# A stored table of places and engines, replaced by another, in a fused attention and gated convolution kernel

## The chip, the cores and the metric

The kernel runs on one core of a Trainium2 chip. The metric is the time of one execution on the device in microseconds (us), as a median of several runs. A profile shows one execution, on the engines PE (matrix products; PEld is its loading of weights), DVE (VectorE), ACT (ScalarE), POOL (GpSimd), and SP, which here issues the transfers (DMAs).

## The reference, cut to what matters

```python
# q, k, v: (8, 8, 576, 64), float32
scores = q @ k.T / 8 + bias                 # bias: (8, 576, 576), the same for each batch
attn = softmax(scores); x = attn @ v        # x joined over the 8 heads: (8, 576, 512)
# bias[h,i,j] = relu(log1p(|i-j|) / log1p(max(i,1)) * w1 + b1) @ w2   (32 hidden units)
gate = sigmoid(causal_conv_of_5_taps(x, conv_w))
out = (gate * (x @ w_val)) @ w_out
```

## The kernel before, in words

The work is cut into 4,041 tasks, each a closure that issues one or a few instructions. It falls into three kinds. **Bias stage**: for 36 bands `b0` to `b35` of 16 rows of the bias, four `relu` tasks per band (one on ACT, L319, the other three on DVE or POOL, L321), products on PE (`bias_mm`, L340), evacuations of the product from PSUM with the constant added (`bias_fin`, on ACT L359 or on DVE L361; one forward and one mirrored piece), and a store to DRAM. **Attention**: 32 pairs `p0` to `p31` of two heads of one batch. A pair has four blocks `c0` to `c3` of 128 queries, and every second pair a block `c4` for the 64 rows that remain of two pairs. A block has `qkm` on PE (L714; `qkr`, L730, for c4), two `logits` on DVE (L760), two `expo` on ACT (L772). Pairs 0 to 5, 24 and 25 normalise the exponentials (`norm`), transpose them on PE (L919) and copy them from PSUM (`tev`, on ACT or DVE). The 24 others split each block into two halves of 16 bits: `top` (copy of the upper half, ACT L197, DVE L199 or POOL L201), `rest` and `rest8` (the subtraction that gives the lower half, 1024 and 128 columns, L220), and then a transposing DMA that SP issues (`swap`, L953, into a tile `t_pt`). `piece` tasks (L986) multiply the transposed block with v. **Gated part**: per batch, `taps`, `conv`, `prod` and `acc` for the convolution, `val` (L1251) and `outp` (L1317) on PE, with their copies and subtractions (`ghi`, `glo`, `ote`) on ACT, DVE or POOL.

What sets the order is no scheduler: the string constant `ORDER`, unpacked, gives for every place of the program the number of a task and the number of its engine among those that the task allows. Each engine gets its instructions in this order and works them off in it; slots of buffers are given out in it too. These lines do it, and the second group is what `bias_fin` allows:

```python
for lo, hi in zip(code[:n], code[n:]):
    t = self.tasks[(lo + 256 * hi) // 4]
    assert not t.done and all(d.done for d in t.deps)
    t.on, t.done = t.engines[lo % 4], True
...
f = add(
    [("A", 0.2 + 0.19 * (hi - lo) / 288), ("V", 0.1 + 0.31 * (hi - lo) / 288)],
    partial(bias_fin, j=j, lo=lo, hi=hi, back=back),
```

Of the kernel before, what the change touches and what calls it, by code (L numbers as in the profile page):

```python
# [1489 lines left out]
```

## Time and profile before

| | before |
|---|---|
| median of 3 runs | 660.95 us (663.14, 660.22, 660.95) |
| span of the profiled execution | 656.1 us |
| median of the runs less this span | 4.85 us |
| PE busy in the span | 618.3 us (94%) |
| DVE busy | 591.6 us (90%) |
| ACT busy | 573.2 us (87%) |
| POOL busy | 496.4 us (76%) |

The span runs from the first to the last instruction of the profiled execution; that execution's own time stands nowhere, so the runs' median is what its 4.85 us around the span are taken from. Busy shares are means over the span: they say which engine has the most work, not which one is waited for in a given stage.

### The profile page before, as it was taken

The page shows a single profiled execution, that of the slowest core. Times are in us where ns is not written, and L with a number is a line of the kernel's source. Part 1 is how long each engine was busy: PE and PEld are TensorE (multiplying, and loading weights), DVE is VectorE, ACT ScalarE, POOL GpSimd, SP SyncE. Part 2 cuts the span into 40 slices and gives each one's busy share as a digit, 9 for nine tenths or more (in the row PEclk, how much of TensorE's full clock was granted, in tenths as well). Part 3 has the DMA queues.
Part 4 walks back from the last instruction along what each step waited for, and adds up shares of the span by engine and source line. Part 5 has one row for each costly group of instructions (what it writes and reads, how often), then busy time and mean ns, then how long its engine had stood idle before and what let it go on. Part 6 is the DMA issues. An engine that isn't in the chain of part 4 may idle for free.

```text
span 656.1 us, 16807 instructions
## 1 busy us (share of the span) xinstructions
PE 618.3 (94%) x6176; PEld 401.5 (61%) x6176; DVE 591.6 (90%) x1594; ACT 573.2 (87%) x1284; POOL 496.4 (76%) x566
## 2 busy tenths in 40 slices
PE   5778999999799999999989999999999999999997
PEld 2223666766566676657556676666676664766673
DVE  7999999999999799899898988998988988899882
ACT  6999999999999999899688998889889877999671
POOL 6576839675798888888888778987878957888630
PEclk9979999999999999999999999999999998999999
DMA  6889957338999999999999999999974999999622
GB/s 193 260 278 344 338 204 212 102 115 149 168 238 195 200 230 197 230 225 199 219 190 233 210 208 212 217 217 181 221 188 116 157 224 170 210 193 172 121 81 96
DMA packets 279106, 129.76 MB, mean 198 GB/s; under 512 B 255600, under 2 KB 255856, under 8 KB 279024
## 3 DMA queue, kind: packets, MB, share of 16 engines
q1 hardware_dynamic: 278880, 128.40, 89.5%
q8 instruction: 48, 0.79, 0.5%
q14 instruction: 34, 0.28, 0.2%
q10 hardware_dynamic: 144, 0.29, 0.1%
HBM read 44.64 MB, written 20.33 MB: 99 GB/s over the span
## 4 chain that ended last, share of the span: by engine, by line
PE 63%; DMA 12%; ACT 10%; POOL 6%; DVE 4%; issue 2%; SPq 1%; DVEq 0%; POOLq 0%; ACTq 0%
PE t_sp L714 16%; PE t_ps L986 13%; PE t_ps L1317 11%; DMA t_pt<-t_d 11%; PE t_ps L1251 10%; PE t_ps L919 5%; POOL t_d L220 4%; ACT t_d L772 3%; ACT t_be L359 2%; PE t_sp L730 2%; DVE t_d L760 2%; PE t_ps L1060 2%; PE t_ps L340 2%; ACT rel L319 2%; ACT t_d L197 1%
## 5 line engine op out<-in xcount | busy, mean ns | idle before, releaser
L220 POOL TENSOR_TENSOR t_d<-t_d,t_d 128x1024 f16<-128x1024 f32 (+1 forms) x178 | 242.8, 1382 | 44.1 <-ACT t_d L197 39.0
L772 ACT ACTIVATE t_d<-t_d,nm 128x576 f32<-128x576 f32 x288 | 221.6, 771 | 22.2 <-DVE nm L760 21.6
L760 DVE CUSTOM_DVE_ANT_0 t_d<-t_sp,bias 128x576 f32<-128x576 f32 x256 | 186.5, 752 | 24.8 <-PE t_sp L714 19.3
L714 PE MATMUL t_sp<-t_qk 64*128 64x288 f32 x1024 | 168.1, 429 | 4.0 <-DVE nm L760 3.4
L986 PE MATMUL t_ps<-t_pt,t_w 128*64 128x256 f16 (+1 forms) x1664 | 122.4, 296 | 8.4 <-DMA t_pt<-t_d 6.0
L714 PEld LDWEIGHTS t_sp<-t_qk 64*128 64x128 f32 x1024 | 95.2, 186 | 49.7 <-DVE nm L760 14.0
L197 ACT CAST t_d<-t_d 128x576 f16<-128x576 f32 x155 | 99.7, 666 | 15.4 <-DMA t_pt<-t_d 9.5
L1251 PEld LDWEIGHTS <-wv 128*128 128x128 f16 x768 | 72.4, 98 | 29.9 <-issue 10.5
L986 PEld LDWEIGHTS <-t_w 128*64 128x64 f16 x1344 | 70.3, 110 | 25.2 <-issue 14.8
L1251 PE MATMUL t_ps<-xh,wv 128*128 128x256 f16 (+1 forms) x480 | 68.4, 286 | 0.0
L1183 DVE SCALAR_TENSOR_TENSOR t_ps<-t_xp,convw,t_ps 128x288 f32<-128x288 f32 x126 | 64.6, 517 | 1.3
L1317 PE MATMUL t_ps<-wo,gh 128*128 128x512 f16 x240 | 59.2, 387 | 0.0
L772 ACT ACTIVATION_READ_ACCUMULATOR t_d<-t_d,nm 128x1 f32 x288 | 55.1, 191 | 0.0
L340 PE MATMUL t_ps<-rel,w 128*32 128x280 f32 (+17 forms) x352 | 40.6, 531 | 11.2 <-ACT t_be L359 6.4
L834 POOL TENSOR_SCALAR t_d<-t_d,rinv 128x576 f32<-128x576 f32 x57 | 42.3, 754 | 10.5 <-DVE rinv L806 9.9
L321 POOL TENSOR_SCALAR rel<-gt,ip,nb 128x560 f32<-128x560 f32 (+11 forms) x17 | 38.7, 2281 | 13.1 <-PE t_ps L340 12.6
L321 DVE TENSOR_SCALAR rel<-gt,ip,nb 128x544 f32<-128x544 f32 (+17 forms) x91 | 46.1, 569 | 0.2
L201 POOL TENSOR_SCALAR t_d<-t_d 128x576 f16<-128x576 f32 x46 | 33.9, 740 | 14.7 <-ACT t_d L772 10.8
L919 PE MATMUL t_ps<-ident,t_d 128*128 128x128 f32 x324 | 43.3, 278 | 1.6 <-POOL t_d L834 0.8
L919 PEld LDWEIGHTS t_ps<-ident,t_d 128*128 128x128 f32 x324 | 35.2, 140 | 13.8 <-issue 5.5
L197 ACT COPY t_pt<-t_ps 128x512 f32<-128x512 f32 (+1 forms) x83 | 36.6, 486 | 4.7 <-PE t_ps L919 4.2
L1317 PEld LDWEIGHTS <-gh 128*128 128x128 f16 x240 | 22.6, 100 | 29.0 <-issue 7.8
(156 smaller groups left out, 1082.4 us busy)
## 6 DMA issues: line engine op xcount, KB each, us to landing
t_qk<-qkd SPq DMA_DIRECT2D x32, 576.0 KB, 4.7
bias_d<-t_be SPq DMA_DIRECT2D x36, 295.5 KB, 4.5
bias<-bias_d SPq DMA_DIRECT2D x16, 576.0 KB, 7.1
out<-t_w SPq DMA_DIRECT2D x32, 256.0 KB, 2.6
t_w<-vd SPq DMA_DIRECT2D x24, 320.0 KB, 3.7
t_w<-vn SPq DMA_DIRECT2D x8, 320.0 KB, 4.4
...
```

What stands on the lines that cost most here:

```text
L197: A.copy(out=out, in_=in_)
L220: (V if e == "V" else G).tensor_tensor(out=out, in0=in0, in1=in1, op=ALU.subtract)
L321: (G if e == "G" else V).tensor_scalar(out=rel[g].t[:, 0:w], in0=src, scalar1=sct[:, mm : mm + 1], scalar2=nb1, op0=ALU.mult, op1=ALU.max,)
L340: T.matmul(pb[32 * g : 32 * g + 32, 0 : y - x], lhsT=w28, rhs=rel[g].t[:, x:y], start=True, stop=True, tile_position=(0, 32 * g),)
L714: T.matmul(ts[a][:, j, 0:hw], lhsT=qk.t[r, c * P : (c + 1) * P], rhs=qk.t[r, x : x + hw], start=True, stop=True,)
L760: V.tensor_tensor_reduce(out=part(c, a).rearrange("p (j f) -> p j f", j=2), in0=sp.t[:, :, 0 : S // 2], in1=bias.rearrange("p (j f) -> p j ...
L772: A.activation(out=part(c, a), in_=part(c, a), func=AF.Exp, bias=nms[c][:, a : a + 1], scale=-1.0, accum_out=sums[c][:, a, 0:1],)
L919: T.transpose(t[:, k * P : (k + 1) * P], es[c].t[:, (k0 + k) * P : (k0 + k + 1) * P], ident)
L986: T.matmul(po.t[r, 0:256], lhsT=vt.t[:, v, r], rhs=pt[:, x, :, :] if tr else pt[:, :, x, :], start=(t == 0 and m == 0), stop=(t == 4 and m ...
L1183: V.scalar_tensor_tensor(out=o, in0=x, scalar=wt, in1=t, op0=ALU.mult, op1=ALU.add)
L1251: T.matmul(pm.t[:, 0:w], lhsT=weights["wv"][wi][:, k, d * P : (d + 1) * P], rhs=xb.t[xi][:, k, 0:w], start=(q == 0 and k == 0), stop=(q == ...
L1317: T.matmul(pm.t, lhsT=gb.t[gi][:, k, o : o + P] if o < 256 else gx.t[gi][:, k, :], rhs=weights["wo"][wi][:, k, :], start=(q == 0 and k == ...
```

## The change

Only the constant `ORDER` differs; no task, tile or pool is changed. Of its text one line of each:

```diff
 ORDER = (
-    'c-mE10cbL3nx6mvCuWjNl1UsBlT7}MagvP5Bu<jiOp?i8yV%7p7VP1IJ?vr+yLgK|>|zgl*uz~cSg?l$d$`~o7VP1FxQl!EFLtqD!5;2m7jN;v1-sbAJ?vq@1$VLF9`}A@ckk|<`M&RcpZ9s+_jBf(ZzjPAx+#*B$FFbT3`exQ*Y!JJ0B=j3MwspPf)U=<Y&-j{S384Ylr0p?rHb7Vi@O|eCEd<$Ae2gHpAS}R;lbE5Y-V!A'
...
+    'c-nPW4{RdWnaA0I9ou7jY!B<PJ=lXiwg-D`#_O?nY|rLMMJiGeiJVA9P9&lya-t`4Vk>eYCwihMB2kH)*b_O?ik^r>Ppm{LTCo+W$cad#;wn;+6RD^~PHaRf_QXn5q7|vg>Ap93x7F$HW9Gf@`+dLf_ul+_Gq^-tLr^3~d+Uv6tKD&Xx)>8N_4<P->kImo({qdcPN-IIHmo^Y%hq-j^M%q|j+nDtN%;KFr(J<$suz3^8uW*FIMN#}#wg;Q'
...
```

Unpacked, 271 of the 4,041 tasks get another engine, and most tasks move by a few to some dozens of places. The constant is two lines shorter, so every line number after it is lower by 2 in the changed kernel (L361 becomes L359, L953 becomes L951).

The first place is DVE in the bias stage, from the `relu` of band 5 on (`rel<-gt,ip,nb`; the last number of a row is its columns). Before, a stretch with no evacuation (`t_be<-t_ps,cadd`):

```order
L321 TENSOR_SCALAR rel<-gt,ip,nb_133 128x416 x3
L321 TENSOR_SCALAR rel<-gt,ip,nb_133 128x480 x3
L321 TENSOR_SCALAR rel<-gt,ip,nb_133 128x464 x2
L321 TENSOR_SCALAR rel<-gt,ip,nb_133 128x400 x3
L321 TENSOR_SCALAR rel<-gt,ip,nb_133 128x352 x3
L321 TENSOR_SCALAR rel<-gt,ip,nb_133 128x304 x3
L423 TENSOR_SCALAR t_w_257<-t_d_256 128x512
L321 TENSOR_SCALAR rel<-gt,ip,nb_133 128x336 x2
```

On the same engine now, over the same bands:

```order
L319 TENSOR_SCALAR rel<-gt,ip,nb_133 128x416 x3
L359 TENSOR_SCALAR t_be<-t_ps_219,cadd 128x95
L319 TENSOR_SCALAR rel<-gt,ip,nb_133 128x480 x3
L319 TENSOR_SCALAR rel<-gt,ip,nb_133 128x464 x2
L359 TENSOR_SCALAR t_be<-t_ps_180,cadd 128x264
L319 TENSOR_SCALAR rel<-gt,ip,nb_133 128x352 x2
L319 TENSOR_SCALAR rel<-gt,ip,nb_133 128x400
L319 TENSOR_SCALAR rel<-gt,ip,nb_133 128x352
L359 TENSOR_SCALAR t_be<-t_ps_168,cadd 128x432
L319 TENSOR_SCALAR rel<-gt,ip,nb_133 128x336 x2
```

Three evacuations of 95, 264 and 432 columns that were ACT's stand on DVE. In the whole stage 14 go from ACT to DVE (3,842 columns) and 6 from DVE to ACT (815 columns); DVE has 20 in place of 12. Of the `relu` tasks 10 go from DVE to POOL and 8 from POOL to DVE.

The second place is SP's queue where pairs 15 and 17 meet (`t_pt` is the target of a `swap`; `out<-` a store of the output; `t_w<-vd` a load of v). Before, with pair 15's last two swaps into `t_pt0`, and pair 17's into `t_pt1`:

```order
L1335 DMA out<-t_w8_258 128x512
L953 DMA_TRANSPOSE t_pt0_896<-t_d3_591 128x18x128
L641 DMA t_w8_258<-vd 128x640
L953 DMA_TRANSPOSE t_pt1_943<-t_d4_711 128x18x128
L953 DMA_TRANSPOSE t_pt0_896<-t_d5_825 128x18x128
L953 DMA_TRANSPOSE t_pt1_943<-t_d6_850 128x18x128
```

The same tasks now, with pair 15 in `t_pt1` and pair 17 in `t_pt0`:

```order
L951 DMA_TRANSPOSE t_pt1_966<-t_d5_791 128x18x128
L951 DMA_TRANSPOSE t_pt1_966<-t_d2_356 128x18x128
L1333 DMA out<-t_w2_189 128x512
L639 DMA t_w4_213<-vd 128x640
L951 DMA_TRANSPOSE t_pt0_908<-t_d6_849 128x18x128
L951 DMA_TRANSPOSE t_pt0_908<-t_d1_211 128x18x128
```

Pair 15's second swap (blocks c3) now stands directly behind its first, ahead of the store, the load and pair 17's first swap.

## Rows read from the trace of the kernel before

**Rows 1.** The page's busy us, share of the span, instructions.
```profile
PE 618.3 (94%) x6176; PEld 401.5 (61%) x6176; DVE 591.6 (90%) x1594; ACT 573.2 (87%) x1284; POOL 496.4 (76%) x566
```
**Rows 2.** Windows: length, busy us of PE, PEld, DVE, ACT, POOL, clock, DMA share, GB/s.
```profile
5.00:80.00 75.00, 61.91 (x513) 26.66 (x515) 74.14 (x186) 70.64 (x153) 54.80 (x48) 0.95 0.87 291
80.00:145.00 65.00, 64.97 (x580) 45.81 (x582) 63.27 (x191) 62.65 (x159) 44.44 (x64) 1.00 0.51 171
145.00:205.00 60.00, 54.68 (x576) 37.68 (x573) 58.93 (x160) 56.99 (x128) 48.02 (x49) 1.00 0.95 177
205.00:300.00 95.00, 94.85 (x934) 62.76 (x933) 85.66 (x223) 88.49 (x194) 80.31 (x89) 1.00 1.10 216
300.00:420.00 120.00, 112.54 (x1256) 76.46 (x1257) 109.07 (x307) 102.25 (x227) 100.39 (x108) 1.00 1.09 209
420.00:607.00 187.00, 184.20 (x1954) 124.13 (x1951) 167.62 (x462) 166.01 (x377) 151.22 (x184) 0.99 0.96 188
```
**Rows 3.** Waits of PE: total us, times, longest.
```profile
PE t_ps L340 <- ACT t_be L359: 6.4, 8, 2.2
PE t_ps L986 <- DMA t_pt<-t_d: 6.0, 9, 2.2
```
**Rows 4.** DVE's evacuations by shape (busy us, mean ns), and one in its place.
```profile
L361 DVE TENSOR_SCALAR t_be<-t_ps,cadd 128x287 f32<-128x287 f32 x1 | 0.5, 497 | 0.0
L361 DVE TENSOR_SCALAR t_be<-t_ps,cadd 128x16 f32<-128x16 f32 x1 | 0.2, 216 | 0.0
...
32.11 0.44 DVE L361 TENSOR_SCALAR t_be<-t_ps,cadd 128x224 f32<-128x224 f32 x1
32.47 2.14 DVE L321 TENSOR_SCALAR rel<-gt,ip,nb 128x368 f32<-128x368 f32 x4
```
**Rows 5.** The relu groups on DVE and POOL, and two stretches of the timeline.
```profile
L321 DVE TENSOR_SCALAR rel<-gt,ip,nb 128x320 f32<-128x320 f32 x6 | 2.3, 435 | 0.0
L321 DVE TENSOR_SCALAR rel<-gt,ip,nb 128x576 f32<-128x576 f32 x5 | 2.7, 574 | 0.0
L321 DVE TENSOR_SCALAR rel<-gt,ip,nb 128x464 f32<-128x464 f32 x5 | 3.4, 721 | 0.0
L321 DVE TENSOR_SCALAR rel<-gt,ip,nb 128x544 f32<-128x544 f32 (+17 forms) x91 | 46.1, 569 | 0.2
L321 POOL TENSOR_SCALAR rel<-gt,ip,nb 128x560 f32<-128x560 f32 (+11 forms) x17 | 38.7, 2281 | 13.1 <-PE t_ps L340 12.6 <-DVE rel L321 0.3
...
27.69 3.42 DVE L321 TENSOR_SCALAR rel<-gt,ip,nb 128x384 f32<-128x384 f32 x9
...
51.61 2.67 DVE L321 TENSOR_SCALAR rel<-gt,ip,nb 128x576 f32<-128x576 f32 x4
...
50.75 4.62 POOL L321 TENSOR_SCALAR rel<-gt,ip,nb 128x576 f32<-128x576 f32 x2
```
**Rows 6.** Copies and subtractions that change engine.
```profile
L199 DVE COPY t_pt<-t_ps 128x512 f32<-128x512 f32 x8 | 5.5, 684 | 0.5 <-PE t_ps L919 0.4
L359 ACT ACTIVATE t_be<-t_ps,cadd 128x272 f32<-128x272 f32 (+29 forms) x68 | 31.2, 530 | 2.4 <-PE t_ps L340 2.3
L220 POOL TENSOR_TENSOR t_d<-t_d,t_d 128x128 f16<-128x128 f32 x87 | 47.7, 548 | 1.1 <-ACT t_d L197 0.5
L220 DVE TENSOR_TENSOR t_d<-t_d,t_d 128x128 f16<-128x128 f32 x21 | 8.4, 402 | 0.0
```
**Rows 7.** SP's queue and PE around 340 us.
```profile
331.33 3.00 SPq L953 DMA_TRANSPOSE t_pt<-t_d  x1
...
335.19 10.70 SPq L953 DMA_TRANSPOSE t_pt<-t_d  x3
...
345.37 1.72 PE L986 MATMUL t_ps<-t_pt,t_w 128*64 128x256 f16 x28 [2.22 <-DMA t_pt<-t_d]
```
**Rows 8.** PE's wait ahead of the last fall of its clock, and a window over it.
```profile
543.41 2.03 PE L714 MATMUL t_sp<-t_qk 64*128 64x288 f32 x8 [1.34 <-DVE nm L760]
...
545.00:549.00 4.00, 4.00 (x13) 1.46 (x11) 3.72 (x12) 2.93 (x8) 3.83 (x6) 0.57 1.08 242
```

More of the change, by code (lines that the diff above doesn't have):

```diff
@@ new lines @@
+    'VV_R2HLPC2g{rfgjfNREK6u$P*5pRxVm|RUnX)<ToKwS#KahkUmt1a7PF5_vVX<HEVw@MVQmuDOvG)h@cao#KDO)AYzb_6Y0Uu{%JxS0trNXc^`zKS4dh3O1`<YIa%XVRgPMU4G@OH;X1$`XhU!+GLz8naKdVF};e=QIie1~B?qi~HqZVHkdQ7m06=FCRDw3UmFH8Dq{K2Efn8h0iaPo_*SIX}&|yXj1)lk0i>j(omQE>`$r;ni>6DIFiW'
+    '+@Yu>TO;o&xW)E<IOd^}bB}moKvFcrCE^KhisgqRLG&3!e^8PIk^NRBLfEpwWYykHV_cOAHeIq}KMRFp@u<Z*cBC@ttkdPj$a{nYCj-N+wke{T%9A+x)1Oc@>#-|VTO;%g=Xm~wRRh!Nl)CNm!&<ZDj5XZezQ-5$2kPxkH<?NdOzG^yMDq7RO*kF$W^xgnz$&A7G%pk~aH3PCq9nG;P8<#|Hm;VdmP)OjPc%A|P3{kd*&mlPF51m{vfiS@'
@@ new lines @@
+    '>GtLPjKY;oR(tP}$K@OO$2AR{)JP>i7`^)YK)oq6TD~CB4plo?_{~B|lqzzg+O!Y~X~oHN#Zt1BtCYP~C$N|uf6EfK+8kDU*MC3oUN|z=1f$_lY_;|sC*yjvQu72qV%?FLH{@&h!-1Mr6UC&erCf<b;)!G`oy}SDg<{;nwQRi?o3>1}P>MKQ6-ar~!~QD+yBrx;Z%1pf1g{Z9uiyF7AW;9J(rCJCje1b>1wy%eyW2^|y`ElkI2vpEzJdlD'
+    'aIIl`^u2T@+Zp4erh6ab@o<!&R{ix-Ifv&1!FY?v6w=uunPCd$Hbqyn^<2J4po={YC1MXBb+}{+BiP@BYYn{2R}4m$BYPIB&=1?}4k2~?FC%%N&wLV%i?^kgtXS=SES4BL$Ju<*mMgTorQX{e9?m^4rs#ko$X^6QmJh8po5ML6ii+UyIMs)fjM&o|mO1;1)#j31Zm+xRd!bIPHeAgplNc4Vc{Y|S6<%{DTOO}(%n5dPfYZDt#reOKD_(!l'
@@ new lines @@
+    'rET|)tGT?p<iWq6&b%H9_&UGo55gLF+J}W=xiX^0IN|k${J#s(!O*wE+!xiFZ;)+b49oFzG!x;qtk5dzqlzHKEOC3Hovb(Tls^#eSRMZ^rZZnkwn&f<MU$Gkr;^HkJ??UsBZVTFNPDy0bWX8YZ4ud*B*;ugOl4z+_>T(3T)r2TS$nZmE!Qg5S{)9x9qWb@l|uBrom?poM;`ADV|7O>-D$f-!WZ+Cfj9$m)?kV9Fq6!5(fr4qe&ewD>(jxA'
+    '`fm+Jm)Q}QEo4)<p(gKedT3_E;+?j;2E&#3ZprH!jk!*nuM=d;<7u?ZAAG4lMANf7N8MjN`s}dh9^b`3Pqy%??9vckj7&L1$g<u?gCQplT-2)gkcVYN^7#X9INScQOa;kN`t~#Zq1)#O`870Qow|*YI2DPeVqBq^&XfY-0Amlw|A|gAyd=o4KN?8o>_FV9RPW`Lu*LeucZRlb#Ac5NN6}y;8jB}V&RV@8B$BaYXguY@(q4Dd=kepb#mPEa'
@@ new lines @@
+    'mUt>%B`KDpqe*!3EBQ>eP%P!j`NEyo2{Ke|#A**2zFDj>az)A5ER|BZUd3w4aieN~_O2lQ`OD5)s_BvBp*N5neQA9ul<P}gC(cr^@`t=WyFZ{fd|{`B@Q2{B4bss-%oTPABN2}$VvE{eh`r^E#Z&5wqnp5Rcp#X6izhRQWFl2{MHA6bEKOHxon$7JO~Yko3#D?+U3BI0g>Jpm$QJK|=ZF`}^-8@}h4Yiu<dVI9syj$G+pR&68q<shYxhDA'
+    'qHHDnADw3FAI6zjykE+H{<|K&Q{~*8r@%|aQkkT9L6j7tKOBt`N$*(03xu4`$Yi#FS!jl}<{dUZo6on2l(WF$wYtk*zt^ai%5CAN?|lHvZvC~P#rh4(+w6E+U0=B|!Wzw9A0D|+#<)gA3$m?or`Mk+sp^32Hd~#_P_zc=khfxkfxE46xBXw$^VPmxsSQ}g@mpVS#0;N___6+I0195l=Vv+lDDbR(jPrq`<G<Aq*y0-+jCVMkFucd>e~wB@'
@@ new lines @@
+    'aw;1Pg(Fd4%^pa<vkHq$43<$>Ji*j5$!tEy<3qTSC^k#GQ}qJe7;^e0w<RYkl0|8%_sg!~t89uFtTv0sYxjNJs>lwT+hhG&+u>|_TuJXMaHDDxUMv}Lc7)@!FIY^K%3}0RDD4l}Q!<CX0J^a_9!wV!lE>c@2bHMT_4n@YMxudlz78)dDU|H{hwuUjhhd_{OePE0uvGf62KOqgpzUO=TrIZasj?@LQSL<wwGL7FWusXtr#t;_Z!jFGPwR*n'
+    'Yp|>(JH$zAktV(*8Jq3-QeNZ0D7%XbP%Pu*Y0fR2vn@PMj+3tZy<lWSKH!C%LRm6a8*T6Avjq`OM$OI0@PIc$xuPW+j<Kg@ukS}cE7w2Jl#;1d!;hZLAXakn?O%QNR=I}LpDT%8rCM)r)pSP?;VXa{Sji^E!s`ITN!ixx4e37N7)fQW|7%yELcye;ec}1B=EdAl=?|p*SYyF#l~A<?cZIfYXWG_gp=D#aI*pb|vB0-wqG4<o_l0BO`64a}'
@@ new lines @@
+    'R);eT4@WrW>oh}=mOmcpMyUAeONM9|oykZvY8heH#5f`LUVbzc3rqfycVK((6rL-%q)fE^;+%_hlY%|z!HKGagCpYpIh7{&DRgK00=$%C1zA*L=p~tf(b55b&E}-Do`Buuuvla};|)99kzmO6{iw(3^1fpAc<-cr{s(BiZM1^!CKb$tqOoke9ge{jEv4y<CW7UOfGy-H2P=gT?&GrATs439+y01{lq|Vadh*zJ{xOm4)CyKPmB@4lKP`33'
+    'CFOocy~e{a;i~ugwqcL#^CP#fOnGX4`wRKl$79W3eJdzbdhtT47)~~QwXtRZYk2{d@zJn4#!|&fJX3F_qcJBD4B_cgGNa+)^^i3tBJZT}X7=6yZxcnfQ!iD!t&h1r2_IXTq@f4jI6H^^0fvt&weO9of&;yxS)QbZ<*df(S-qG40>kGt#fnP{=de_%i|tmUnWJcq$qSRmJYcoE>2@|4@$xe35twT9v{fK`$C6FRdE32MJWxm|WD(9%IZ3ha'
@@ new lines @@
+    '!Xr_Ypqzj33z_NG<Fb%f6wAl50xy1eu)TitsL00&LF{`vU5n2i8ECA}73|Vju{tzPSF;o>6QPPs(!-G@_f-chuZl%-x(LcmS3RLf*~Zw6c`s+T2BMa**6Me9-cG&h^ZC<+ZN!SMeS6U1_&O|smG9yoL<`kA`cCNfW3Z~$LgDw^5l>R^xx9_Js3`X;r4M6?nl#W1`8YOG@G;EqmmXhGkQVQ}AzS<bxN0BnBpUiv1C|ZvtdYE!95*wmZsiB?'
+    'rnzmYXNMXgV>DrSqxP@m%2?xtMZX4bz~Cpg<9e&no*(>r@r_!$+4-#d@F6~I*>miUW>lpePKMO;VYEbH*3PF9!O^b?GUfR4&3DDS&L7VZWJ+;~-9o9~d!P0c2lnCU%)z*7b<XYdx_<DC^|^-R?#qMQ<8N5d73K2vAp2%)c>fCxkJ)4KbQ0b9@j|Ga$Vf@M!`<yQsh0E84$YOq*6&q{B_~e2^4CB22WpXeAfN7LgS`*~H*m1t=r>v3(@q`o'
@@ new lines @@
+    'WV9tpwoWJ-{tI}*<a8us%eHcZSa@iMHLh5ybg6L<9;0~K+4i`+#lqdH0&AZA?RGE}g-;Hq&${q|`++3@{}r6WRJizY(>Le0lHb_<!Zbjin*pICO0kGL^^b|HD;P<4AHLm8x4M~JAluLVtn%{^7OmCcmc`+o72#uq@Jd|IBZp&oU)v(U6ykRu`0Y8R;V5;yzLY;1PDP^W^e8tDWcq{OmEVk6<<~<QSQ!=D{a7iRX*4_PS1PB7Ba5c|mK}4j'
+    '*=|e1ll5{tZcS9~j&V8npD)4TwblFInk;qt*!z{<ANWVlJ2YKQwK5=jgQ}(1$FVL!(U^_&{GJ(&hwd6Yt#Gd?Xn_rcC|V=16{mY_vDbpHcD-Nt>fuHZX9<$ytFTCse$HVH*_^__VR5=NwU0h&HK+~tMOS<0HQvR$dvd3Xk%2@rEF>e7Pam{64e(^OF`w?e*|PFOicTFfQjDdWeYYV0c4&y#Y<E8%ds3cXwvy?|tH_ftdn-k#Y~Bo{eT8gJ'
@@ new lines @@
+    'EPdLMyxiZ|`#~vGgwGX3`?iv9B$AoeN4}vS?gCFMV*kps4)`o-zc~8gbN9Tq`z04FVI{a@1Lew>p|R#Cv0~3RtafUjzx>f3{x0e+cY@7O9DVaxDb8l+8JZ2FPY~JS7{g=j|86f*i+7`eemD`qaEgu%;zMSX_~F~>QsLbS!8VGi%)N4}!8Th-9G#?bwAvKv?bH-@EXmXwqhu_w5SJ^~uh|{#^k-eN`iqa8UY{%fllyK@58mP!T-g5LPH>tq'
+    'aO`lTd19Dq&|d|b|HG!9^vIi<f_~~x!>K3Dv{r}fX7I=CsR{nn)YMb3<Ip~(Mcxzwo|<^jKJIbd1Xr7Ds)IfC#HLjI+SD~5!~T@2i4Yur>e@B6;u;S7HB5I6`DjCi&_6X)0sD32WAH<pP78+)F%B)J(}AbEro%A&+T`?HLp|&`j{VV444qD^)nV7M>(_A<U%#%?;aVJ+VArpM0)8D-R9)Do=KzERJ~7=iYNw~CuY;q#vg_KJX<UnFT9g69'
@@ L79 @@
+    'W~e+>4I;Fio|%DrCY=GvbZR!6RKEFCh7|HnPtR1k`OGZCiGbK7tCN+?qS-9VAS6Qvxk<tK=_y1am{~j*&FAJxY(7I&S(Hx^DkA3Dxp*pykb^v+=VvNYmd{RM1G;>Eb`H_RE<o_?{NfCh&k=rs!1HtYT!eb@;u2tSVt}cVP$^zqAo}_F#RaNSUDcozip7ibi*r>D7?(&-gb~E^Gf=s>B7y|cK0`GZ7q`x#L0V^Lm$xp#Kmj4DkZP9~SB4yr'
+    'yu3UE$x9J+m$y{AxOEHQ3sio2OF@W&s23mz{iT`%{+Xg&-U8OGD@g^N0p&tb6aX)7DUiQ)sa#$vw}1y+AOZk0m_!qO;3}7oM^cc=C6oaHHboUv$5#-n+`gL5Z4{`6GH1$d<%%~k;N4a`HG=kORC`MV|4;4dtNxb!B%DC#+B^-u{DdOQk87UTRms!;pUM9#{xf7(jttKK0OOCY0s'
 )
```

38 lines of the change are left out of this document (8 added, 30 removed).

## The prediction

> **What bounds the kernel now.** I read three views: the busy times, the windows by stage, and the waits of PE. The page gives PE 94% and DVE 90% of the span [rows 1], but a mean hides stages, so the windows decide. They fall into two parts [rows 2]. From 5 to 205 us DVE is busy 74.14 + 63.27 + 58.93 = 196.3 of 200 us; all its idle time there is 3.7 us. PE has 18.4 us of it. An engine that works its list off in order and is idle for 3.7 us in 200 cannot be hurried by relieving another: whatever work DVE is given ahead of 205 us moves everything behind it, up to what those 3.7 us take. From 205 to 607 us PE is the fullest (391.6 of 402 us) and DVE has 39.7 us free; behind 607 us PE works off the last batch. What PE can win back behind 205 us is its idle time: 0.2 us to 300, 7.5 us from 300 to 420, and 2.8 us from 420 to 607. The waits of PE put names to it [rows 3]: evacuations by ACT in the bias stage (6.4 us), and transposed blocks that have not landed (6.0 us). The first is no loss of its own, since DVE is full there anyway; the second is.
>
> Nothing of what the kernel computes is removed, so the change is a sum over tasks that changed engine and over places where one engine waits. I count tasks until about 205 us, where DVE stops being the bound.
>
> **Evacuations of the bias, DVE +4.2 us.** 14 go from ACT to DVE with 3,842 columns, 6 back with 815. On DVE a piece of 224 columns holds the engine from 32.11 to 32.47, 0.36 us, and 16 and 287 columns last 216 and 497 ns, a slope of 1.04 ns a column [rows 4]. At their mean of 274 columns the 14 cost 14 x 0.41 = 5.8 us; the 6, at 136 columns, give back 6 x 0.27 = 1.6. ACT is relieved of a net 8, which last 530 ns in the mean [rows 6], so by about 4 us. But ACT has 4.4 us idle from 5 to 80 us where DVE has 0.9 [rows 2].
>
> **Relus, DVE +0.2 us.** 10 go to POOL (4,320 columns), 8 come back (3,760). Alone, they last 435 ns at 320 columns and 574 at 576, and nine of 3,088 columns in all take 3.42 us [rows 5], so each holds DVE about 0.08 us less than it lasts. That gives 4.2 us removed and 3.5 added, net -0.7. POOL gets two more, and these are not free to DVE: the four relus from 51.61 on, 1,968 columns in all, would take 2.0 us alone and take 2.67 beside POOL's, and the 464-column group lasts 721 ns, longer than 576 columns alone. All 91 on DVE (39,648 columns) come to 38.2 us at the lone price; they are busy 46.1 us with 17 on POOL. That is 7.9 / 17 = 0.46 us of DVE for each relu on POOL, so two more cost 0.9.
>
> By the Trainium skill's page "SBUF — State Buffer", section "Who interferes with whom", a DVE instruction in a two-port mode and a GpSimd instruction lock each other out for the whole instruction. The rows show less: nearly every DVE relu beside POOL's runs on, and one or two per POOL relu are held up for some 0.3 us.
>
> **Other tasks ahead of 205 us, DVE +1.2 us.** Of pairs 0 to 5, three copies of 512 columns and two of 128 go from ACT to DVE, and one of 512 comes back: 684 ns less the overlap, 0.6 us, for the wide ones [rows 6], and an estimated 0.25 by the slope of rows 4 for the small, 1.7 us in all. Small sums of the softmax, some `top` and some `rest8` go both ways; with each group's mean they net between -1.2 and +0.3 us, depending on where one cuts. I take -0.5.
>
> DVE thus has 5.6 us more to do ahead of 205 us. The 3.7 us of idle time bound the delay from below: 1.9 us if none is left, 5.6 us if all stays. ACT's relief should close some of these gaps; I take 1.6, so **+4.0 us** at 205 us. PE has the same work ahead of that point as before (no product group moves past it for good), so the delay passes to PE whole, and PE then has no slack in which to repay it but its own waits.
>
> **Swaps, -2.2 us.** At 345.37 PE starts pair 15's second half after 2.22 us idle, waiting for a transposed block [rows 7]. SP did swap c2 of this pair at 331.33 for 3.00 us, then a load, and from 335.19 on three swaps in 10.7 us, of which pair 15's c3 is the second. It now stands directly behind c2, at 334.3 in place of 335.19 + 3.57 = 338.8: 4.4 us sooner, more than PE's wait. Behind it are the store, the load and pair 17's first swap, some 3.6 us later than before; pair 17's products come later than all of this, so nothing new waits at once. I take the whole 2.22 us; none is the other end, if POOL's `rest` is late.
>
> **What is hidden.** Over the whole program 11 more `rest8` go to DVE: 402 ns each there, 548 on POOL [rows 6], +4.4 and -6.0 us, nearly all behind 205 us. DVE has 39.7 us free from there to 607 us [rows 2], so I cost it at nothing; without this cover, up to +1 us in the full stretches from 205 to 300 us. PE's clock falls to its lower level, 1.2 GHz, for part of 545 to 549 us (mean 0.57 [rows 8]), after PE had waited 1.34 us for DVE's logits; at most 4 x 0.43 = 1.7 us hang on it. A new order can lose this fall or get another, so 0, and 1.7 us either way for the range. What the clock falls ahead of 80 us (mean 0.95 [rows 2]) lies under a full DVE.
>
> **Sum.** +4.0 - 2.2 = +1.8 us. The span is 656.1 us, the runs' median 660.95, 4.85 us more; against the median this gives 662.75, rounded to **662.7 us**.
>
> **Rivals.** A change of 0.5% is 3.3 us, about what a measurement here can tell from none: 657.65 to 664.25.
>
> A: *the waits from 300 to 420 us go* (faster). PE idles 7.5 us of 120 there, against 2.8 us of 187 behind [rows 2]. If the new places of swaps and `rest8` bring it to that rate, 1.8, PE wins 5.7 us; with the least delay on DVE, 1.9, that is -3.8, so 657.2, and 655.5 if the clock's fall goes too. For it: POOL, on which the swaps wait, is busy 84% in that stretch and loses work. Against: only one of these waits have I followed to an order that removes it. It decides from 3.3 us above DVE's delay on.
>
> B: *the delay is not repaid* (slower): +4.0 to +5.6 with no gain at 345 us, since another block is late in its place: 665.0 to 666.6. For it: from 300 to 420 us SP does a swap nearly without pause, 10.70 us for three [rows 7], and what is brought forward pushes another back. Against: pair 17 has time.
>
> C: *POOL's relus lock DVE for their whole length*. Each would then cost up to its 2.28 us [rows 5], two more 4.6 rather than 0.9: 662.7 + 3.7 = 666.4, or more. It is the page's rule above; the lone and the crowded durations speak against it.
>
> Chances: my forecast, with 659 to 664 as its own range, 0.38; A 0.29; B 0.28; C 0.05. Faster 0.29, same 0.38, slower 0.33. The range from 655.0 to 667.5 takes in A down to where a clock's fall goes with it, and B and C up to their prices, and leaves out 0.2.
>
> **What would show it.** In the windows of the changed kernel, DVE is busy for all but 2 us from 5 us to where pair 9 begins its third block, and this point comes 2 to 6 us later than before; DVE's whole busy time is about 600 us. If it comes no later, the count of DVE's work is wrong, or ACT was waited for after all. The relu groups would stay near 0.46 us of loss per POOL relu. PE's wait before pair 15's second half is gone and its wait for `t_pt` is under 6.0 us; if it is as large as before, another swap is late. PE's idle time from 300 to 420 us decides between my forecast and A. The prediction is wrong if DVE's full stretch is no chain: if part of what it does ahead of 205 us could wait, and the new table lets it.

## The result, and the profile after

The changed kernel takes 668.75 us (median of 9 runs, 667.01 to 669.69); the kernel before, run beside it, 661.83 (9 runs, 660.22 to 666.44). The ratio is 1.0095, 95% interval 1.007 to 1.012: slower by 0.95%, where 662.7 was forecast and 667.5 was the upper end of the range. Of the three rivals, B (the delay is not repaid, up to 666.6) and C (POOL's relus lock DVE, 666.4 or more) had the right sign.

The profiled execution took 668.32 us, its span is 666.5: 1.8 us lie around the span. Of the 4.85 us that the forecast put around the span of before, some 3 us were therefore chance: that one execution was faster than any of the nine runs. Five later traces of kernels that do the same things up to pair 5 put pair 0's block c2 1.3 to 2.0 us later than the trace behind [rows 2]. Differences between the two traces (10.4 us at the end) overstate the change by as much.

The page of the changed kernel, its busy line:

```profile
PE 626.6 (94%) x6176; PEld 400.0 (60%) x6176; DVE 611.8 (92%) x1627; ACT 565.0 (85%) x1261; POOL 494.5 (74%) x556
```

DVE has 20.2 us more to do than in [rows 1]; the forecast said about 600. The same stretches as in [rows 2], of the changed kernel, the end split at 577 us, where pair 30 begins, and a piece of 2 us:

```profile
5.00:80.00 75.00, 63.24 (x483) 24.76 (x483) 73.21 (x178) 64.62 (x136) 53.63 (x44) 1.00 0.82 266
80.00:145.00 65.00, 64.23 (x570) 43.38 (x569) 61.83 (x190) 61.48 (x155) 45.07 (x66) 1.00 0.56 187
145.00:205.00 60.00, 53.00 (x525) 37.28 (x523) 58.91 (x154) 54.99 (x124) 48.35 (x51) 0.97 0.81 171
...
182.00:184.00 2.00, 1.98 (x14) 0.50 1.08 205
...
300.00:420.00 120.00, 115.89 (x1227) 75.58 (x1226) 113.15 (x305) 103.80 (x227) 93.46 (x94) 1.00 1.10 212
...
577.00:607.00 30.00, 28.36 (x288) 18.71 (x286) 28.93 (x65) 25.91 (x57) 22.78 (x26) 1.00 0.91 181
607.00:656.00 49.00, 46.75 (x480) 31.64 (x476) 41.06 (x98) 26.36 (x54) 25.41 (x37) 1.00 0.50 98
```

From 5 to 205 us DVE is busy 193.95 of 200 us: its idle time rose from 3.7 to 6.1 us, where DVE "busy for all but 2 us" was forecast. Half or more of that rise is the luck of the one trace: in four later traces that have the table of before up to pair 17 or further, DVE idles 4.9 to 5.4 us there. From 300 to 420 us PE idles 4.1 us in place of 7.5. Two windows of before, for comparison with the last two (the changed kernel is 6 to 10 us behind in its work there):

```profile
577.00:607.00 30.00, 29.58 (x360) 21.04 (x359) 27.88 (x71) 28.18 (x62) 24.95 (x29) 1.00 1.02 182
607.00:656.00 49.00, 45.13 (x376) 28.04 (x376) 32.43 (x70) 24.52 (x51) 16.93 (x24) 1.00 0.39 99
```

PE's waits, to set beside [rows 3]:

```profile
PE t_ps L338 <- DVE rel L319: 4.7, 5, 1.6
PE t_ps L984 <- DMA t_pt<-t_d: 4.2, 4, 2.3
PE t_sp L712 <- DVE nm L758: 3.7, 5, 1.7
```

ACT's evacuations are gone from the head of the list, DVE's relus stand there now. The groups that answer to [rows 4 to 6]:

```profile
L359 DVE TENSOR_SCALAR t_be<-t_ps,cadd 128x271 f32<-128x271 f32 (+18 forms) x20 | 8.8, 450 | 0.1
L319 DVE TENSOR_SCALAR rel<-gt,ip,nb 128x576 f32<-128x576 f32 (+16 forms) x89 | 45.6, 568 | 0.2
L319 POOL TENSOR_SCALAR rel<-gt,ip,nb 128x528 f32<-128x528 f32 (+11 forms) x19 | 42.1, 2219 | 13.6 <-PE t_ps L338 11.7 <-DVE rel L319 1.8
L218 DVE TENSOR_TENSOR t_d<-t_d,t_d 128x128 f16<-128x128 f32 x32 | 17.9, 559 | 0.9 <-ACT t_d L195 0.8
```

The last line is the surprise: 32 subtractions of 128 columns at 559 ns each, where 21 lasted 402 [rows 6]. They cost DVE 9.5 us more, not 4.4. Counted over all DVE instructions that subtract or split with both operands in SBUF (L218, L206, L666, L1146), what they lasted above the length of an undisturbed one of the same form comes to 11.4 us before and 24.0 now: 12.6 of DVE's 20.2 us more are such standing time.

The places where PE lost time, from the timelines of the changed kernel (PE, DVE, POOL and SP; start, length, engine):

```profile
179.90 2.89 PE L712 MATMUL t_sp<-t_qk 64*128 64x288 f32 x8 [1.70 <-DVE nm L758]
182.81 2.33 PE L984 MATMUL t_ps<-t_pt,t_w 128*64 128x256 f16 x28
185.07 1.24 PE L712 MATMUL t_sp<-t_qk 64*128 64x288 f32 x8
195.79 0.63 PE L1058 MATMUL t_ps<-t_d,t_w 128*64 128x64 f16 x28 [1.62 <-DVE t_xp L1041]
...
192.12 0.75 DVE L758 CUSTOM_DVE_ANT_0 t_d<-t_sp,bias 128x576 f32<-128x576 f32 x1
192.80 2.60 DVE L666 SCALAR_TENSOR_TENSOR t_w<-t_w,vsc,t_w 128x640 f16<-128x640 f32 x1
195.32 0.41 DVE L1041 TENSOR_TENSOR t_xp<-t_xp,t_ps 128x256 f32<-128x256 f32 x1
...
192.59 2.13 POOL L218 TENSOR_TENSOR t_d<-t_d,t_d 128x1024 f16<-128x1024 f32 x1
...
586.07 2.62 DVE L206 SCALAR_TENSOR_TENSOR xl<-t_xp,bsc,xh 128x512 f16<-128x512 f32 x1
588.62 0.74 DVE L758 CUSTOM_DVE_ANT_0 t_d<-t_sp,bias 128x576 f32<-128x576 f32 x1
...
585.96 3.01 POOL L218 TENSOR_TENSOR t_d<-t_d,t_d 128x1024 f16<-128x1024 f32 x2 [1.25 <-ACT t_d L195]
...
589.42 1.91 PE L712 MATMUL t_sp<-t_qk 64*128 64x288 f32 x8 [1.18 <-DVE nm L758]
612.50 0.84 PE L984 MATMUL t_ps<-t_pt,t_w 128*64 128x256 f16 x12 [2.25 <-DMA t_pt<-t_d]
...
602.75 9.64 SPq L951 DMA_TRANSPOSE t_pt<-t_d  x3
```

Read at 192.80: DVE's lower half of v (L666), which mostly lasts about 0.87 us, stands 2.60 us. POOL's subtraction of 1,024 columns runs beside it until 194.72, and 0.68 us later DVE is done. Behind it on DVE stands L1041, which frees the bank that PE's L1058 waits for: 1.62 us. At 586.07 it is the same with the lower half of x (mostly 0.74 to 0.75 us): POOL's subtraction of 1,024 columns (it ends at 588.14, the row counts the next one in), then 0.55 us, then at last the logits, for which PE waits 1.18 us. At 179.90 PE, after 1.70 us idle, runs at its lower level, 1.2 GHz (mean 0.50 from 182 to 184): 2.89 + 2.33 us for groups that take 1.24 and 1.72 at the upper one [rows 7], so up to 2.3 us lost.

How late the changed kernel is, by the starts of logits in the two traces: +5.1 us at pair 0's block c2 (77 us), +3.7 at pair 8, +8.2 at pair 9, +10.5 at pair 17, +7.7 at pair 16 right behind it, +5.6 at pair 30, +10.4 at the end.

### The profile page after: what moved, and what is told of

Read it like the earlier page. It is cut to its first block, busy times and chain, and to the rows that moved or that the text cites. A ratio compares the mean times of both kernels' runs of the same rounds, so it can differ in the third digit from the quotient of the medians.

```text
span 666.5 us, 16836 instructions
## 1 busy us (share of the span) xinstructions
PE 626.6 (94%) x6176; PEld 400.0 (60%) x6176; DVE 611.8 (92%) x1627; ACT 565.0 (85%) x1261; POOL 494.5 (74%) x556
## 4 chain that ended last, share of the span: by engine, by line
PE 58%; DVE 19%; DMA 8%; ACT 6%; issue 4%; POOL 3%; SPq 1%; DVEq 0%; ACTq 0%; POOLq 0%
PE t_sp L712 14%; PE t_ps L984 12%; PE t_ps L1249 10%; PE t_ps L1315 10%; DMA t_pt<-t_d 6%; PE t_ps L917 5%; DVE t_d L758 5%; DVE rel L319 5%; PE t_sp L728 2%; ACT t_d L770 2%; DVE t_d L218 2%; PE t_ps L1058 2%; POOL t_d L218 2%; ACT t_d L195 1%; PE t_ps L338 1%
## 5 line engine op out<-in xcount | busy, mean ns | idle before, releaser
L218 POOL TENSOR_TENSOR t_d<-t_d,t_d 128x1024 f16<-128x1024 f32 (+1 forms) x166 | 230.6, 1403 | 62.3 <-ACT t_d L195 46.8
L758 DVE CUSTOM_DVE_ANT_0 t_d<-t_sp,bias 128x576 f32<-128x576 f32 x256 | 185.5, 750 | 16.6 <-PE t_sp L712 11.9
L984 PE MATMUL t_ps<-t_pt,t_w 128*64 128x256 f16 (+1 forms) x1664 | 125.9, 297 | 7.2 <-DMA t_pt<-t_d 4.2
L195 ACT CAST t_d<-t_d 128x576 f16<-128x576 f32 x151 | 96.5, 666 | 9.8 <-DVE t_d L218 2.7
L832 POOL TENSOR_SCALAR t_d<-t_d,rinv 128x576 f32<-128x576 f32 x56 | 44.0, 798 | 14.7 <-DVE rinv L804 14.0
L338 PE MATMUL t_ps<-rel,w 128*32 128x288 f32 (+17 forms) x352 | 45.1, 491 | 10.1 <-DVE rel L319 4.7
L319 POOL TENSOR_SCALAR rel<-gt,ip,nb 128x528 f32<-128x528 f32 (+11 forms) x19 | 42.1, 2219 | 13.6 <-PE t_ps L338 11.7
L199 POOL TENSOR_SCALAR t_d<-t_d 128x576 f16<-128x576 f32 x51 | 35.4, 699 | 17.0 <-ACT t_d L770 14.3
L319 DVE TENSOR_SCALAR rel<-gt,ip,nb 128x576 f32<-128x576 f32 (+16 forms) x89 | 45.6, 568 | 0.2
L218 DVE TENSOR_TENSOR t_d<-t_d,t_d 128x128 f16<-128x128 f32 (+1 forms) x50 | 40.0, 803 | 1.3 <-ACT t_d L195 1.2
```

The lines of the kernel that those rows point to most:

```text
L195: A.copy(out=out, in_=in_)
L218: (V if e == "V" else G).tensor_tensor(out=out, in0=in0, in1=in1, op=ALU.subtract)
L319: (G if e == "G" else V).tensor_scalar(out=rel[g].t[:, 0:w], in0=src, scalar1=sct[:, mm : mm + 1], scalar2=nb1, op0=ALU.mult, op1=ALU.max,)
L338: T.matmul(pb[32 * g : 32 * g + 32, 0 : y - x], lhsT=w28, rhs=rel[g].t[:, x:y], start=True, stop=True, tile_position=(0, 32 * g),)
L758: V.tensor_tensor_reduce(out=part(c, a).rearrange("p (j f) -> p j f", j=2), in0=sp.t[:, :, 0 : S // 2], in1=bias.rearrange("p (j f) -> p j ...
L984: T.matmul(po.t[r, 0:256], lhsT=vt.t[:, v, r], rhs=pt[:, x, :, :] if tr else pt[:, :, x, :], start=(t == 0 and m == 0), stop=(t == 4 and m ...
```

## The experiments

A kernel here is the table with some entries replaced; what is computed never changes. "Before" was run beside each (medians 660.9 to 662.5 us). Ratios are against it, with 95% intervals.

| kernel | us | ratio |
|---|---|---|
| changed | 668.75 | 1.0095 [1.007, 1.012] |
| e1: its 20 evacuations on the old engines | 671.91 | 1.0156 [1.0113, 1.020] |
| e2: before, with the 20 on the new engines | 668.77 | 1.0118 [1.0066, 1.017] |
| e3: its 25 moved `rest8` on the old engines | 674.85 | 1.0205 [1.0159, 1.025] |
| e4: its places, all engines of before | 739.85 | 1.1192 [1.1136, 1.1249] |
| h1: before to pair 5, then the change | 667.01 | 1.0092 [1.0062, 1.0121] |
| h2: the change to pair 5, then before | 670.24 | 1.0133 [1.0085, 1.0181] |
| t1: the change to pair 30, then before | 662.61 | 1.0005 [0.998, 1.003] |
| t2: before to pair 30, then the change | 667.59 | 1.0067 [1.0035, 1.0098] |
| h3: before, pairs 17 to 29 of the change | 658.65 | 0.998 [0.9945, 1.0016] |
| m1: before, pairs 22 to 29 of the change | 663.0 | 1.001 [0.998, 1.0041] |
| v2: one held instruction moved | 668.02 | 1.0107 [1.006, 1.0155] |
| v3: six held instructions moved | 671.95 | 1.0133 [1.0096, 1.0171] |
| x2: one `rest8` back on POOL | 667.5 | 1.0079 [1.005, 1.0108] |
| x3: five of v3's six, and x2's | 665.75 | 1.0053 [1.0031, 1.0076] |
| x4: h3 with two held instructions moved | 659.63 | 0.9957 [0.9934, 0.998] |

### Engines without their places

```diff
 for t in order_of_change:            # e1; e3 the same with rest8, e4 with every task
-    engine = engine_in_change[t]
+    engine = engine_in_before[t] if kind(t) == "bias_fin" else engine_in_change[t]
 for t in order_of_before:            # e2
-    engine = engine_in_before[t]
+    engine = engine_in_change[t] if kind(t) == "bias_fin" else engine_in_before[t]
```

e1. 

> The changed kernel with the engines of the 20 moved evacuations of the bias as before, nothing else. Theory W (work): DVE works an unbroken chain ahead of 205 us, so the 4.2 us of evacuations that it was given delay all behind them: the time falls by about 4 us, from 668.7 to 664.5 (663.5 to 665.5), and pair 0's block c2 starts some 4 to 5 us sooner than 82.2 us. Theory H (holds): the loss comes from DVE instructions that stand still while a subtraction of 1,024 columns runs on POOL; the evacuations have no part in it, so 668 to 669.5 and the holds on DVE stay. The prediction's sum has 4.2 us here too, with 1.6 of it closed by ACT's relief: 666.

e2. 

> The kernel before with the engines of the 20 evacuations as in the change, nothing else. W: +4 to +5 us against before (661.8), so 666 to 667, with pair 0's block c2 starting 4 to 5 us later than 77.1 us. H: within 1 us of before. If some of the delay is repaid further on, between 662 and 665.

e3. 

> The changed kernel with all 25 moved subtractions of 128 columns on the engine of before, so 11 fewer on DVE. H: the holds of these on DVE (8.7 us in the changed kernel above their free length, 2.5 in the one before) go for the most part, and the time falls by 2 to 6 us, to 663 to 667. The prediction took them as hidden in DVE's idle time behind 205 us, and W says nothing of them: 668 to 669.5, or a little more since POOL gets 6 us of work back.

e4. 

> The places of the change with every task on the engine of before. If engines make the whole loss (W and H together, as far as holds come from engines), about the time before, 660 to 663. If the places make it (holds arise where instructions meet, which places decide as well), 665 to 669.

All four are slower than the kernel they were made from, and theory W falls with the first (e2 by itself goes its way, 7.8 us by ratio where W had 4 to 5). The window from 5 to 80 us and a wait of PE, of e1, then of e2:

```profile
5.00:80.00 75.00, 61.54 (x478) 23.89 (x475) 68.95 (x169) 66.54 (x143) 52.46 (x43) 1.00 0.80 263
...
PE t_ps L338 <- ACT rel L317: 5.4, 8, 1.9
```

```profile
5.00:80.00 75.00, 58.45 (x453) 22.00 (x450) 68.03 (x169) 59.45 (x127) 50.40 (x38) 0.91 0.80 247
...
PE t_ps L339 <- ACT t_be L358: 8.5, 7, 2.6
```

In e1 DVE is relieved of 4.3 us of work in this stretch and simply idles for it: pair 0's block c2 comes at +5.9 us, not at +1. ACT, with its evacuations back at places that were not made for them, is now late with its relus, for which PE waits 5.4 us. In e2 DVE's list is longer and DVE is busy 6 us less than in [rows 2]: PE waits 8.5 us for ACT's evacuations, and DVE for PE. So DVE "full" is not DVE the bound. As I read these rows, two engines and PE hand each other the work of a band, and a change of engine at unchanged places lengthens that round. e4 shows how far it goes: 79 us above before, where at most 669 us was expected. e3 loses 6 us in place of gaining 2 to 6: `rest8` on DVE falls from 17.9 to 12.3 us, but most of this comes back on held lower halves of x (33.8 to 37.6 us), so it says nothing on the 11 `rest8` by themselves.

### Where the table loses: joining the two tables

A joint is made at the first logits of a pair: all tasks ahead of it from one table, what is left from the other.

```diff
-order = change                                   # h1
+order = before[:first_logits(5)] + [t for t in change if t not yet done]
-order = change                                   # t1
+order = change[:first_logits(30)] + [t for t in before if t not yet done]
```

h1. 

> Places and engines of before up to the first logits of pair 5 (124 us), those of the change for everything behind it. Theory P (the start): what the changed table does ahead of that point, places and engines together, costs the 5.4 us by which pair 5 starts later in its trace, and nothing behind gives it back: 668.7 - 5.4, so 663.3 (662 to 665). Rival R (repaid): the two parts are each other's match, and PE or DVE had room for the delay behind it: 667 or more.

h2. 

> The reverse: places and engines of the change up to pair 5, those of before behind it. P: before plus 5.4, 661.5 + 5.4 = 666.9 (665.5 to 668.5). R: 662 to 664.

h3. 

> The table of before, but from the first logits of pair 17 (327 us) to those of pair 30 (571 us) the places and engines of the change. In the two traces the changed kernel is 10.5 us late at the first of these points and 5.6 at the second, so this stretch alone wins 4.9 us: 656.6 (655 to 659), faster than both. Rival: it only wins back what had been lost just ahead, since what came late had room: 660 to 663.

m1. 

> The table of before, with the places and engines of the change from pair 22 (434 us) to pair 30 (571 us) only. The changed trace goes from 8.0 to 5.6 us late over this stretch, so it wins 2.4 us: 658.5 (657 to 660) against 660.9, if the joint at pair 22 costs nothing; the joint at pair 17 in the kernel with the longer middle cost 4 us. If joints cost some us whatever their place: 661 to 664.

t1. 

> The changed kernel up to the first logits of pair 30 (577 us), places and engines of before behind it. Its trace is 5.6 us late at this point and 10.4 at the end, so the table's last 90 us alone cost 4.8: span 661.7, time 663.6 (662 to 665.5). If the end is late because what went before it left POOL and DVE with more to do, 667 to 669.

t2. 

> The reverse of the kernel that ends like before: the table of before up to the first logits of pair 30 (571 us), places and engines of the change behind it. If the last 90 us of the changed table cost what they cost in its own trace, whatever stands ahead: 661 + 4.8 to 6.1, so 666 to 667.5. If they are late only for what the changed table leaves to them (a longer list on DVE and POOL at pair 30): 660 to 663.

t1 and t2 agree: what the changed table does from pair 30 on, its last 90 us, costs 4.4 us behind the table of before and 5.9 us (0.90%) behind its own. With the old end the change is as fast as before. The last two windows of t1, against 28.36 and 46.75 us of PE in the changed kernel, which is 1 us further behind where the first begins and 4 where the second does:

```profile
577.00:607.00 30.00, 30.00 (x347) 20.35 (x343) 28.30 (x71) 28.75 (x63) 25.09 (x28) 1.00 1.05 190
607.00:656.00 49.00, 48.85 (x429) 31.14 (x428) 36.26 (x79) 27.93 (x59) 20.49 (x30) 1.00 0.47 110
```

The start is another matter. At pair 5 the change is 4.9 to 5.8 us late in eight traces that begin like it, and five that begin like before are 1.3 to 2.0 us late against the one trace: some 3.5 us. h2 keeps them and loses 4 more at its joint; h1 avoids them and is not faster for it: its lead in the trace over the changed kernel is 4.1 us at pair 5, 2.3 at pair 30, 1.0 at the end. h1 lands at the edge of what R said (667 or more), h2 above what either said (P up to 668.5): the delay is given back in part, over 450 us. What makes the 3.5 us is not shown.

The middle does gain, as its trace said, but h3 lost 4 of these us at its joint (from +2.9 to +7.1 between pairs 15 and 17), and m1 2 at its own, about what its stretch wins. In the time of h3 what is left, 0.2%, is inside the interval. That joints have a price was foreseen by m1's rival alone, which came true (661 to 664).

### Held instructions

x3 and v3 move these (v2 the first alone):

```diff
 DVE around 192 us (v2, v3, x3)
 L758 ISA t_d_577,nm<-t_sp_404,bias_2_88 128x576
+L666 SCALAR_TENSOR_TENSOR t_w_358<-t_w_359,vsc,t_w_358 128x640
 L758 ISA t_d_577,nm<-t_sp_405,bias_2_88 128x576
-L666 SCALAR_TENSOR_TENSOR t_w_358<-t_w_359,vsc,t_w_358 128x640
 DVE around 235 us (v3 alone): L206, the split of x, ahead of the four tasks before it (taps, a product, logits, taps)
 DVE around 301, 366, 516, 586 us (v3, x3): L218, L218, L218, L206 behind the next 5, 4, 3, 2 tasks
 x2, x3: rest8 of pair 30, block c1
-DVE L218 TENSOR_TENSOR t_d_211<-t_d_849,t_d_211 128x2x64
+POOL L218 TENSOR_TENSOR t_d_211<-t_d_849,t_d_211 128x2x64
```

v2. 

> The changed kernel with two neighbours on DVE exchanged, the lower half of v for pair 8 (L666) and the second logits of block c2 behind which it stood; nothing else moves. It lasts 2.60 us in the changed kernel, 0.88 where nothing disturbs it, and POOL's subtraction of 1,024 columns runs from 192.59 to 194.72 beside it. Theory H: DVE's instruction with both operands in SBUF waits until POOL's ends; begun 0.7 us sooner it comes ahead of that subtraction, lasts about 1.1 us, PE's wait of 1.62 us ahead of L1058 shrinks to under 0.5, and pair 9 starts 1 to 1.5 us sooner: 667.3 (666.5 to 668). If the length comes from anything else (its 640 columns, its operands), it lasts 2.6 us in the new place too and the time is 668.7.

DVE, POOL and PE of v2 at the same place:

```profile
192.41 0.93 DVE L666 SCALAR_TENSOR_TENSOR t_w<-t_w,vsc,t_w 128x640 f16<-128x640 f32 x1
...
192.66 2.68 POOL L218 TENSOR_TENSOR t_d<-t_d,t_d 128x1024 f16<-128x1024 f32 x1
...
194.07 1.23 PE L712 MATMUL t_sp<-t_qk 64*128 64x288 f32 x6 [0.39 <-DVE nm L758]
```

Begun 0.25 us ahead of POOL's subtraction, the same instruction lasts 0.93 us, and POOL's 2.68 in place of 2.13: now POOL stands. PE's wait of 1.62 us is gone, one of 0.39 is new. The mechanism is shown; a gain in time is not (pair 9 starts 0.5 us sooner in the trace and the median is 0.7 lower, but the ratio is higher, 1.0107 against 1.0095), also because PE's clock was low for longer just ahead, from 180 to 187 us.

v3. 

> The changed kernel with six instructions of DVE moved by one to five places of its list, so that none starts beside POOL's subtraction of 1,024 columns: the lower halves of v (192.7 us) and of x (235.5 and 585.9 us), two subtractions of 128 columns (301.4 and 365.8 us) and a subtraction of the gate (515.5 us). No engine changes, and the lists of PE, ACT, POOL and SP are the same. In the changed kernel these six last 2.60, 3.13, 2.24, 2.24, 2.16 and 2.62 us, some 10.5 us above their free lengths. Theory H (holds make the loss): at least half of the holds that stand ahead of logits passes to PE, 668.5 - 4 = 664.5 (662.5 to 666.5). Rival (DVE has room behind 205 us): only the two that PE waits for at 194 and 589 us count, 1.6 + 1.2 us at most, 666 to 668.

It is slower than the changed kernel, by 2.5 us by ratio and 3.2 by the medians (the intervals overlap), where both theories had it faster. Its trace shows a longer hold of the kind that it was to remove. DVE, POOL and PE around the split of x that was moved forward:

```profile
232.92 4.99 DVE L206 SCALAR_TENSOR_TENSOR xl<-t_xp,bsc,xh 128x512 f16<-128x512 f32 x1
...
230.97 2.54 POOL L218 TENSOR_TENSOR t_d<-t_d,t_d 128x1024 f16<-128x1024 f32 x2
233.44 1.43 POOL L1146 TENSOR_TENSOR t_w<-t_w,t_w 128x576 f32<-128x576 f32 x1
234.80 2.53 POOL L218 TENSOR_TENSOR t_d<-t_d,t_d 128x1024 f16<-128x1024 f32 x2
237.29 0.97 POOL L202 TENSOR_SCALAR gtmp<-t_xp,bsc 128x256 f32<-128x256 f32 x1
...
239.40 2.29 PE L712 MATMUL t_sp<-t_qk 64*128 64x288 f32 x6 [3.92 <-DVE nm L758]
```

It had been 3.13 us long at its old place; begun 2.7 us earlier, it met a run of POOL's instructions without a gap and stood until 0.58 us behind the fifth of them, which ends at 237.33: 4.99 us. PE waits 3.92 us, its clock falls again (mean 0.96 from 205 to 300 us), and pair 12 starts 5.3 us later than in the changed kernel. One hold on the chain, 4.25 us above its free length, passed to everything behind it.

x2. 

> The changed kernel with one task on the engine of before: the subtraction of 128 columns of pair 30, block c1, on POOL behind the one of 1,024 columns, no place changed. On DVE it stands idle beside POOL from 596.62 to 598.45 us, and SP, which can do nothing else (its queue is empty from 594.2 to 598.6 us), swaps the block only then; three more swaps follow, and PE waits 2.25 us for the last of them at 610.2. If this hold makes the wait, SP's swap comes 1.5 to 4 us sooner, the wait shrinks by as much, and the time is 668.5 - 2 = 666.5 (665.5 to 667.5). If the wait is made by the logits or by pair 31's own blocks: no change within 1 us.

x3. 

> Five of the six moves of the earlier try (all but the split of x at 235.5 us, which met two of POOL's instructions in place of one and stood 4.99 us), and the one subtraction of pair 30 back on POOL. Theory H: the holds at 194, 301, 366, 516, 586 and 597 us go, which are 1.6, 0.8 to 1.9, 1.3 and 2.2 us of PE's time where PE waits for them, less what meets anew: 668.5 - 4 = 664.5 (662.5 to 666.5). If holds are no cause of the loss, 668 to 670.

In x2 SP's swap starts at 591.80, 6.8 us sooner (the whole trace is 2.4 us ahead there), but PE still waits 1.66 us for the last block:

```profile
591.80 3.21 SPq L951 DMA_TRANSPOSE t_pt<-t_d  x1
...
597.25 12.27 SPq L951 DMA_TRANSPOSE t_pt<-t_d  x3
...
609.56 0.85 PE L984 MATMUL t_ps<-t_pt,t_w 128*64 128x256 f16 x12 [1.66 <-DMA t_pt<-t_d]
```

The three swaps now take 12.27 us in place of 9.64, from the start of the first to the end of the last, so what held the last of them was not this `rest8`. The run is 1.1 us faster by ratio, inside its interval.

x3 is 2.8 us faster than the changed kernel by ratio (the intervals just overlap), within what H gave. Its trace says where: between pairs 30 and 31 it loses 0.8 us against the trace of before, the changed kernel 3.0, and x2, which lacks the move at 586 us, 3.9. PE's product at 588.56 follows without a wait, since the split of x stands behind the logits:

```profile
588.24 0.39 PE L1034 MATMUL t_ps<-ident,rhl 128*64 128x128 f16 x8
588.56 1.24 PE L712 MATMUL t_sp<-t_qk 64*128 64x288 f32 x8
```

Not all holds went: the lower half of v begins at 192.71 in x3, 0.27 us behind POOL's subtraction, and lasts 2.54 us. Standing time as counted above is 22.0 us in x3 and 22.5 in v3, against 24.0 in the changed kernel: most of what was moved came up again elsewhere, so neither run says what the table would take without holds. In t2, which has the end of the change behind the table of before, the hold at 586 us is back (DVE and PE):

```profile
583.99 2.62 DVE L207 SCALAR_TENSOR_TENSOR xl<-t_xp,bsc,xh 128x512 f16<-128x512 f32 x1
...
587.34 2.96 PE L713 MATMUL t_sp<-t_qk 64*128 64x288 f32 x8 [1.79 <-DVE nm L759]
```

x4. 

> The kernel with the changed table from pair 17 to pair 30 (658.7 against 660.9), with the two held instructions of this stretch moved (a subtraction of 128 columns at 366 us and one of the gate at 516 us). H: DVE gets 3 us back, of which PE takes 0.5 to 2: 657.5 (656 to 659), faster than before by 0.3 to 0.7%. If PE is the bound in this stretch and not DVE, no change against that kernel: 658 to 660.

x4 is the one kernel here that is faster than before clear of noise, by 0.43% [0.2, 0.66]; its 659.63 us lie outside what H said (656 to 659) and inside its rival's range. That the two moves did it is not shown: h3 without them is at 0.998, the two traces agree within 0.9 us at every pair (spans 656.4 and 656.6), and their standing times are 16.4 and 16.6 us. What the numbers suggest is that the changed table is better from pair 17 to pair 30; for that stretch without the two moves the interval still takes in no change.

## Why the prediction was wrong, step by step

**Evacuations, +4.2 us of DVE: right in size, wrong in effect.** By each one's hold of the engine DVE's evacuations went from 3.25 to 7.50 us, +4.25; all of DVE's work ahead of pair 9's third block grew by 4.7 us (196.6 to 201.3 us; 5.6 forecast). **Relus**: by the same division as for [rows 5] (39,088 columns at the lone price are 37.7 us), (45.6 - 37.7) / 19 = 0.42 us of DVE for each one on POOL, as forecast; rival C is out for relus. (Alone, the four relus from 51.61 on come to 1.9 us at the prediction's own price, not 2.0; no term rests on it.)

**"An engine that is idle for 3.7 us in 200 cannot be hurried" and "ACT's relief should close 1.6 us": failed.** e1 and e2 show that the stage is no chain on DVE: the work given back became idle time. That DVE had 3.7 us free, from which the bounds of the delay were worked out, was read from the one lucky trace; in others like it DVE idles 4.9 to 5.4. The delay at pair 0 came to about 3.5 us (5.1 against the one trace), near the +4.0, but not for the reason given. At pair 9's third block it is 7.3 us against the trace, above the forecast 2 to 6, and 5.1 to 5.8 against the four traces like before: the hold at 192.80 and the fall of PE's clock at 180 us, 1.6 and up to 2.3 us, lie between.

**Swaps, -2.2 us: the wait went, the gain did not last.** Pair 15's second half starts without a wait, its last block is in place 4.8 us sooner than needed (SP, then PE), and the changed kernel's lag falls by 2.8 us there (10.5 to 7.7):

```profile
334.14 10.89 SPq L951 DMA_TRANSPOSE t_pt<-t_d  x3
...
349.84 0.52 PE L984 MATMUL t_ps<-t_pt,t_w 128*64 128x256 f16 x6
351.42 1.39 PE L984 MATMUL t_ps<-t_pt,t_w 128*64 128x256 f16 x22
```

PE's wait for `t_pt` is 4.2 us. But the lag is 9.5 us at pair 15 and 9.1 again at pair 21 (415 us), so nearly all of it is lost nearby. Rival A falls with that: PE's idle time from 300 to 420 us fell by 3.4 us, but the stretch is shorter by some 0.4. **Clock**: up to 2.3 us lost at 180 us, where before had no fall; the fall at 545 us of [rows 8] is gone (mean 1.00 from 420 to 607 us). Within the 1.7 either way, nearly.

**Nothing costed for the stretch from pair 30 on: this step made the miss.** Up to 607 us the prediction let DVE's 39.7 us of idle time cover what DVE was given, and "behind 607 us PE works off the last batch" had no term. From pair 30 on (571 us in the trace of before) the table costs 4.4 to 5.9 us (t2, t1), and most of it ahead of 607 us: the lag is 5.6 us at pair 30, 8.6 at pair 31, 9.1 at pair 31's last block (607 us) and 10.4 at the end. Of these us some 2 are the hold at 586 us (x3's trace, and its return in t2), for which PE waits: free time of DVE at other places does not help there. The rest is open; PE's 2.25 us of waiting at 610 us are not settled: x2 took away the suspected hold and left 1.66.

With the old end the time is 662.6, what the sum gave, but by errors that cancel: more delay at 205 us than forecast, hardly a gain from 300 to 420 us, and from pair 21 to pair 30 a fall of the lag by 3.5 us (9.1 to 5.6) that no term foresaw.

**"11 more rest8, +4.4 us, hidden by 39.7 us free": mis-sized, and not all hidden.** They cost 9.5 us, since POOL holds them up, and DVE's whole busy time is 611.8 us and not about 600. Much of it was hidden all the same: from pair 13 to pair 30 DVE is busy 278.8 us in place of 273.4, and the stretch takes 301.4 us in place of 302.9. x3 does not decide it: it moves two held `rest8` and a `glo` there, but DVE's busy time falls by 1.1 us only and the stretch by 0.8.

**The rule that was set aside.** The prediction weighed one sentence of the Trainium skill's page "SBUF — State Buffer", section "Who interferes with whom", against the relus, and found it too strong there, as it is. By another sentence of the Trainium skill in that section, a DVE instruction with two SBUF inputs contends with a GpSimd instruction that reads SBUF. The runs agree with it: 0.93 and 2.60 us for one and the same instruction. It bears on `rest8`, `glo` and the lower halves of v and x, and was not weighed. In v3 the hold went on through further instructions of POOL: its 4.99 us are longer than any one of them. For these instructions rival C's mechanism, a DVE instruction that stands as long as POOL's runs, was the right one.
